# Turning q and k of chunks 4 to 11 by DMA transposes in place of TensorE, in a fused attention and feed-forward kernel

## The chip, the cores and the metric

One core of a Trainium2 chip. The experiments ran in three sets on three chips, and each ratio is to runs of the kernel before in the same set. The metric is device microseconds of one execution; lower is better.

## The reference

Attention over 4 batches, 8 heads, 768 positions, head size 64. A query sees the 8 global keys and the last 96 positions, with a distance bias per head. Its output, 3072 tokens by 512, goes through a feed-forward layer with a squared ReLU. Inputs and output are float32; the kernel computes in float16 with float32 sums.

```python
scores = scale * np.matmul(q, k.transpose(0, 1, 3, 2))
keep = is_global | ((rel >= 0) & (rel < n_local))          # 8 global keys, 96 local ones
scores = np.where(keep, scores + bias, -1e9)
a = softmax(scores)                                        # cut: written out in the reference
x = np.matmul(a, v).transpose(0, 2, 1, 3).reshape(3072, 512)
h = np.maximum(x @ w_in, 0.0)                              # w_in 512 x 2048
out = h * h @ w_out                                        # w_out 2048 x 512
```

## The kernel before

The work is cut into 12 chunks of 256 tokens. For each chunk the kernel loads q, k and v (GpSimd queue, cast to float16), turns q and k so that the head dimension lies on partitions, scores, attends, turns the attention output (`to_x`), and runs the two feed-forward products `first` and `second`. All engines but SyncE follow a fixed order: `place` puts the side jobs of a later chunk (attention, the turns) into numbered slots between the main feed-forward jobs.

The turn of q is eight 128x128 TensorE transposes into one PSUM bank, one ScalarE copy of 128x1024 to SBUF (the eviction), and two VectorE copies across partition halves. The turn of k is the same, followed by four small VectorE copies that build the keys of the neighbouring chunk.

```python
def turn_q(c, h0=0, h1=H, by=None):
    ck = chunks[c]
    ...                                     # cut: allocation of ck.q
    trp = bank([P, H, P], "trq", FP16)
    for h in range(h0, h1):
        nc.tensor.transpose(out=trp[:, h, :], in_=ck.sq[:, h, :], identity=ident)
    hh = slice(h0, h1)
    (by or nc.scalar.copy)(out=ck.q[:, 1, hh, :], in_=trp[:, hh, :])
    def beside():                           # runs just before the next job
        nc.vector.tensor_copy(out=ck.q[0:HP, 2, hh, :], in_=ck.q[HP:P, 1, hh, :])
        nc.vector.tensor_copy(out=ck.q[HP:P, 0, hh, :], in_=ck.q[0:HP, 1, hh, :])
    later.append(beside)
...
for c in range(1, NC):                      # one chunk period
    if c + 5 < NC:
        load(c + 5)
    main = zip_jobs(f2(c), f1(c + 1)) if c + 1 < NC else f2(c)
    side, slots = [], []
    if c + 3 < NC:
        side = [att[c + 3][i] for i in ORDER]
        slots = [0, 4, 5, 7, 8, 11, 12, 15]
    if c + 4 < NC:
        side += prep(c + 4) + [lambda c=c: fix_v(c + 4)]   # prep: turn_q, turn_k
        slots += [2, 9, 13]
    run(place(main, side, slots))
```

The softmax here doesn't subtract the row's maximum and nothing guards it: scores larger than these inputs give would overflow.

## Time and profile before

| | |
|---|---|
| median time | 240.03 us (239.79 to 240.20, 4 runs) |
| span in the profile | 239.2 us |
| TensorE, VectorE, ScalarE busy | 93%, 64%, 60% |
| period of one chunk, 80 to 185 us | 17.55 us |

The profile page of the kernel before. The first part gives busy time, share of the span and instructions. The rows of tenths cut the span into 40 slices of 6 us. The row that begins with 82% is the chain of work that ended last.

```profile
span 239.2 us, 5383 instructions
PE 221.9 (93%) x2214; PEld 155.1 (65%) x2214; DVE 152.4 (64%) x409; ACT 143.6 (60%) x256; POOL 38.6 (16%) x51
...
PE   4666988979899999999999999999999999999993
...
DMA  6999999994968159158249110110110111101112
...
q1 hardware_dynamic: 3456, 6.29, 6.8%
...
PE 82%; ACT 8%; DVE 6%; DMA 2%; issue 1%; POOL 0%; POOLq 0%
```

TensorE is full from about the twelfth slice to the end (busy 10.00 us in every stretch of 10 us from 70 to 230 us), and the chain is TensorE's. The DMA engines are busy for nine tenths or more from the second slice to the ninth, to about 54 us, while the weights and first chunks come in, and then busy in bursts. So each us of TensorE issue time after 70 us is a us of the kernel; other engines' work counts only where TensorE waits for it.

The groups of instructions that the change touches, in the kernel before: busy us and mean ns of one, then idle time before them.

```profile
L207 ACT COPY kx<-trk 128x1024 f16<-128x1024 f16 x11 | 11.8, 1069 | 0.8 <-PE trk L205 0.8
L192 ACT COPY qx<-trq 128x1024 f16<-128x1024 f16 x11 | 11.6, 1054 | 1.6 <-PE trq L190 1.6
...
L205 PE MATMUL trk<-ident,sk 128*128 128x128 f16 x96 | 8.2, 234 | 0.4 <-DMA sk<-in_k_dram 0.4
L190 PE MATMUL trq<-ident,sq 128*128 128x128 f16 x96 | 8.2, 234 | 2.0 <-DMA sq<-in_q_dram 2.0
```

A mean of 234 ns is not what a transpose costs: matmuls overlap, and the eight of one batch took 0.61 us together, not 8 x 0.234 = 1.87. The cost is what a batch delays. In the timeline of the kernel before (start, duration, instruction), the batch starts at 98.75 us and the next matmul at 99.19:

```profile
97.88 1.04 PE L329 MATMUL hps<-xt,w_in_sb 128*128 128x256 f16 x8
...
98.75 0.61 PE L190 MATMUL trq<-ident,sq 128*128 128x128 f16 x8
...
99.19 1.03 PE L341 MATMUL yps<-w_out_sb,h 128*128 128x512 f16 x4
```

That is 0.44 us for eight transposes, 55 ns each. One more place matters: the first period's handover to chunk 4, in the same timeline. The brackets give TensorE's idle time before an instruction and what ended it.

```profile
58.58 0.65 DVE L195 COPY qx<-qx 64x1024 f16<-64x1024 f16 x1 [0.69 <-ACT qx L192]
...
59.76 0.28 PE L304 MATMUL trx<-perm,tm 128*128 128x128 f16 x2
60.40 0.28 PE L304 MATMUL trx<-perm,tm 128*128 128x128 f16 x2 [0.36 <-DVE tm L292]
...
61.36 0.23 PE L261 MATMUL sp<-qx,kx 64*128 64x128 f16 x2 [0.67 <-ACT xt L306]
```

TensorE waited 0.36 us for tm and 0.67 us for ScalarE's xt, which came late because its own matmul had waited for that tm.

### The profile page before, as it was taken

Reading aid. Unit: us, or ns where it says so; the run is one execution under the profiler, and the core shown is the slowest. Engines: PE = TensorE matmul, PEld = TensorE weight load, DVE = VectorE, ACT = ScalarE, POOL = GpSimd, SP = SyncE. Lnnn points to the kernel's source line nnn. Section 1 sums busy time; section 2 is a strip of 40 time slices with the busy share of each in tenths; the row PEclk is TensorE's granted clock in tenths of the full one; section 3 lists DMA queues with packets and bytes.
Section 4 is the critical chain, followed back from the end, with each engine's and each line's share of the span. In section 5 each row is a group of like instructions: output and inputs, shape, how many; then the busy total and the mean of one; then the engine's idle time right before and its main releaser. Section 6 shows DMA issues by size and latency. Waiting matters only on the chain.

```text
span 239.2 us, 5383 instructions
## 1 busy us (share of the span) xinstructions
PE 221.9 (93%) x2214; PEld 155.1 (65%) x2214; DVE 152.4 (64%) x409; ACT 143.6 (60%) x256; POOL 38.6 (16%) x51
## 2 busy tenths in 40 slices
PE   4666988979899999999999999999999999999993
PEld 1554776846567767777676777767766676766651
DVE  7676689766967765567768755658758564333231
ACT  2975996957755764864764774784684564233310
POOL 8842534212302102102102000000000000000000
PEclk9999999999999999999999999999999999999998
DMA  6999999994968159158249110110110111101112
GB/s 61 192 193 203 192 207 187 182 181 83 167 98 84 51 89 91 48 87 88 57 79 90 44 47 0 47 45 3 44 47 0 47 45 47 43 1 47 44 44 88
DMA packets 45144, 20.26 MB, mean 85 GB/s; under 512 B 37952, under 2 KB 42048, under 8 KB 45120
## 3 DMA queue, kind: packets, MB, share of 16 engines
q0 software_dynamic: 41664, 13.63, 51.0%
q1 hardware_dynamic: 3456, 6.29, 6.8%
q8 instruction: 17, 0.28, 0.5%
q14 instruction: 7, 0.06, 0.1%
HBM read 27.26 MB, written 6.29 MB: 140 GB/s over the span
## 4 chain that ended last, share of the span: by engine, by line
PE 82%; ACT 8%; DVE 6%; DMA 2%; issue 1%; POOL 0%; POOLq 0%
PE yps L341 34%; PE hps L329 33%; PE sp L261 5%; PE av L285 4%; ACT ex L268 4%; PE trx L304 2%; DMA sq<-in_q_dram 2%; PE trq L190 2%; PE trk L205 2%; ACT hr L332 2%; DVE tm L292 1%; ACT kx L207 1%; ACT qx L192 1%; DVE qx L195 1%; DVE qx L196 1%
## 5 line engine op out<-in xcount | busy, mean ns | idle before, releaser
L329 PE MATMUL hps<-xt,w_in_sb 128*128 128x256 f16 x768 | 101.1, 276 | 0.0
L341 PE MATMUL yps<-w_out_sb,h 128*128 128x512 f16 x384 | 97.3, 379 | 0.0
L332 ACT ACTIVATE hr<-hps 128x512 f16<-128x512 f32 x96 | 58.9, 617 | 62.3 <-PE hps L329 58.0
L329 PEld LDWEIGHTS <-w_in_sb 128*128 128x128 f16 x768 | 72.7, 99 | 18.5 <-issue 0.2
L333 DVE TENSOR_TENSOR h<-hr 128x512 f16<-128x512 f16 x96 | 40.5, 422 | 43.9 <-ACT hr L332 43.4
L268 ACT ACTIVATE ex<-sp 128x512 f16<-128x512 f32 x96 | 49.4, 609 | 8.3 <-PE sp L261 8.3
L341 PEld LDWEIGHTS <-h 128*128 128x128 f16 x384 | 34.8, 98 | 26.6
L271 DVE TENSOR_TENSOR phat<-ex,mask 128x1024 f16<-128x1024 f16 x48 | 33.0, 691 | 20.7 <-ACT ex L268 20.7
L285 PEld LDWEIGHTS <-phat 128*128 128x128 f16 x384 | 18.8, 101 | 8.6 <-DVE phat L271 2.0
L292 DVE TENSOR_TENSOR tm<-av,rec 128x256 f16<-128x256 f32 x48 | 20.4, 425 | 1.7
L285 PE MATMUL av<-vodd,phat 128*128 128x65 f16 x256 | 18.5, 201 | 2.5 <-DVE vodd L238 1.5
L345 DVE COPY y<-yps 128x512 f32<-128x512 f32 x24 | 16.4, 685 | 5.4 <-PE yps L341 5.4
L306 ACT CAST xt<-trx 128x512 f16<-128x512 f32 x24 | 14.6, 608 | 8.5 <-PE trx L304 8.5
L261 PE MATMUL sp<-qx,kx 64*128 64x128 f16 x256 | 15.5, 232 | 2.9 <-DVE kx L207 1.3
L178 POOL DMA_DIRECT2D sq<-in_q_dram x12 | 10.7, 892 | 44.6 <-PE trq L190 40.3
L261 PEld LDWEIGHTS <-kx 64*128 64x128 f16 x256 | 10.5, 100 | 9.3 <-issue 6.8
L178 POOL DMA_DIRECT2D sk<-in_k_dram x12 | 10.5, 876 | 33.9 <-PE trk L205 29.1
L304 PE MATMUL trx<-perm,tm 128*128 128x128 f16 x96 | 10.6, 226 | 4.7 <-DVE tm L292 4.7
L304 PEld LDWEIGHTS <-tm 128*128 128x128 f16 x96 | 7.3, 99 | 8.8 <-DVE tm L292 6.2
L192 ACT COPY qx<-trq 128x1024 f16<-128x1024 f16 x11 | 11.6, 1054 | 1.6 <-PE trq L190 1.6
L207 ACT COPY kx<-trk 128x1024 f16<-128x1024 f16 x11 | 11.8, 1069 | 0.8 <-PE trk L205 0.8
L285 PE MATMUL av<-veven,phat 128*128 128x65 f16 x128 | 11.3, 194 | 0.0
(55 smaller groups left out, 132.5 us busy)
## 6 DMA issues: line engine op xcount, KB each, us to landing
out_dram<-y SPq DMA_DIRECT2D x24, 256.0 KB, 2.0
sq<-in_q_dram POOLq DMA_DIRECT2D x12, 256.0 KB, 6.3
sk<-in_k_dram POOLq DMA_DIRECT2D x12, 256.0 KB, 6.9
sv<-in_v_dram POOLq DMA_DIRECT2D x12, 256.0 KB, 7.5
w_in_sb<-in_moe_w_in_dram POOLq DMA_DIRECT2D x4, 512.0 KB, 12.2
w_out_sb<-in_moe_w_out_dram POOLq DMA_DIRECT2D x4, 512.0 KB, 17.2
```

Of the source, the lines that this page charges most:

```text
L178: nc.gpsimd.dma_start(out=dst, in_=src[ck.b, :, ck.u * CH:(ck.u + 1) * CH, :].rearrange("h (p e) d -> p h (e d)", e=2))
L261: nc.tensor.matmul(sp[ek][:, e, s, :], lhsT=ck.keys[rr][rows, h, :], rhs=ck.q[rows, 1 - ek:3 - ek, h, rr * HP:(rr + 1) * HP], start=True, ...
L268: nc.scalar.activation(out=ex[:, ek].rearrange("p e c -> p (e c)"), in_=sp[ek].rearrange("p e s c -> p (e s c)"), func=AF.Exp, scale=scale)
L271: later.append(lambda: nc.vector.tensor_tensor(out=phat, in0=ex, in1=mask[:, :, 2 * a:2 * a + 2, k0:k0 + 2, :].rearrange("p k e s c -> p k ...
L285: nc.tensor.matmul(av[:, e, rr, :], lhsT=phat[:, ek, e, s * P:(s + 1) * P], rhs=ck.vals[rr][:, 2 * a + e, ek, 0:D + 1], start=ek == 0, sto ...
L292: nc.vector.tensor_tensor(out=tm.rearrange("p r e d -> p e r d"), in0=av[:, :, :, 0:D], in1=rec[:, :, :, None].to_broadcast([P, 2, 2, D]), ...
L304: nc.tensor.matmul(trx[:, i, rr, :], lhsT=ck.tm[2 * g + i][:, rr, :, :], rhs=perm, start=True, stop=True)
L329: nc.tensor.matmul(hps[:, m2, :], lhsT=w_in_sb[:, kk, m * P:(m + 1) * P], rhs=ck.xt[:, kk, :], start=kk == 0, stop=kk == NCT - 1)
L332: nc.scalar.activation(out=hr, in_=hps, func=AF.Relu)
L333: later.append(lambda: nc.vector.tensor_tensor(out=ck.h2[:, 2 * i:2 * i + 2, :], in0=hr, in1=hr, op=ALU.mult))
L341: nc.tensor.matmul(ck.yps, lhsT=ck.h2[:, m, j * P:(j + 1) * P], rhs=w_out_sb[:, m, :], start=m == 0, stop=m == NFT - 1)
L345: nc.vector.tensor_copy(out=y, in_=ck.yps)
```

## The change

The intent is to take these transposes off the engine that bounds the kernel. For chunks 4 to 11, q and k are turned SBUF to SBUF by DMA transposes on SyncE's queue, which also carries the output stores. A pair is issued at the start of the period before the one that uses it, one to one and a half chunk periods ahead; loads are written one step earlier to match, and SyncE's queue gets a fixed order like the others.

```diff
+    def turn_dma(c):
+        ck = chunks[c]
+        new_q(c)
+        new_k(c)
+        nc.sync.dma_start_transpose(out=ck.q[:, 1], in_=ck.sq.rearrange("p h c -> p (h c)"))
+        nc.sync.dma_start_transpose(out=ck.k, in_=ck.sk.rearrange("p h c -> p (h c)"))
 ...
     def prep(c):
-        return [lambda: turn_q(c), lambda: turn_k(c)]
+        if c < NPE:                                      # NPE = 4
+            return [lambda: turn_q(c), lambda: turn_k(c)]
+        return [lambda: fix_q(c), lambda: fix_k(c)]      # VectorE copies only, as before
 ...
+    engines = {PE, ..., mybir.EngineType.SP}
 ...
-        load(5)
+        turn_dma(4)
+        load(6)
+        turn_dma(5)
         run(place(f2(0), ...))
         for c in range(1, NC):
             if c + 5 < NC:
-                load(c + 5)
+                turn_dma(c + 5)
+            if c + 6 < NC:
+                load(c + 6)
```

More of the change, by code (lines that the diff above doesn't have):

```diff
@@ L180, in load @@
                     "h (p e) d -> p h (e d)", e=2))
-    def turn_q(c, h0=0, h1=H, by=None):
-        ck = chunks[c]
-        if h0 == 0:
-            ck.q = qk_p.tile([P, 3, H, P], FP16, name="qx", tag="qx")
-        trp = bank([P, H, P], "trq", FP16)
-        for h in range(h0, h1):
-            nc.tensor.transpose(out=trp[:, h, :], in_=ck.sq[:, h, :], identity=ident)
-        hh = slice(h0, h1)
-        (by or nc.scalar.copy)(out=ck.q[:, 1, hh, :], in_=trp[:, hh, :])
-        def beside():
-            nc.vector.tensor_copy(out=ck.q[0:HP, 2, hh, :], in_=ck.q[HP:P, 1, hh, :])
-            nc.vector.tensor_copy(out=ck.q[HP:P, 0, hh, :], in_=ck.q[0:HP, 1, hh, :])
-        later.append(beside)
@@ L199, in turn_k, with new_q @@
-    def turn_k(c, h0=0, h1=H, by=None):
-        ck = chunks[c]
-        if h0 == 0:
-            ck.k = kx_p.tile([P, H, P], FP16, name="kx", tag="kx")
-        trp = bank([P, H, P], "trk", FP16)
-        for h in range(h0, h1):
-            nc.tensor.transpose(out=trp[:, h, :], in_=ck.sk[:, h, :], identity=ident)
-        hh = slice(h0, h1)
-        (by or nc.scalar.copy)(out=ck.k[:, hh, :], in_=trp[:, hh, :])
+    def new_q(c):
+        chunks[c].q = qk_p.tile([P, 3, H, P], FP16, name="qx", tag="qx")
@@ new lines, in new_k, with turn @@
+    def new_k(c):
+        chunks[c].k = kx_p.tile([P, H, P], FP16, name="kx", tag="kx")
+    def turn(st, dst, h0, h1, by):
+        trp = bank([P, H, P], "trp", FP16)
+        for h in range(h0, h1):
+            nc.tensor.transpose(out=trp[:, h, :], in_=st[:, h, :], identity=ident)
+        (by or nc.scalar.copy)(out=dst[:, h0:h1, :], in_=trp[:, h0:h1, :])
+    def turn_q(c, h0=0, h1=H, by=None):
+        if h0 == 0:
+            new_q(c)
+        turn(chunks[c].sq, chunks[c].q[:, 1], h0, h1, by)
+        later.append(lambda: fix_q(c, h0, h1))
@@ new lines, in turn_k, with fix_q @@
+    def turn_k(c, h0=0, h1=H, by=None):
+        if h0 == 0:
+            new_k(c)
+        turn(chunks[c].sk, chunks[c].k, h0, h1, by)
+        later.append(lambda: fix_k(c))
+    def turn_dma(c):
+        ck = chunks[c]
+        new_q(c)
+        new_k(c)
+        nc.sync.dma_start_transpose(out=ck.q[:, 1], in_=ck.sq.rearrange("p h c -> p (h c)"))
+        nc.sync.dma_start_transpose(out=ck.k, in_=ck.sk.rearrange("p h c -> p (h c)"))
+    def fix_q(c, h0=0, h1=H):
+        ck, hh = chunks[c], slice(h0, h1)
+        nc.vector.tensor_copy(out=ck.q[0:HP, 2, hh, :], in_=ck.q[HP:P, 1, hh, :])
+        nc.vector.tensor_copy(out=ck.q[HP:P, 0, hh, :], in_=ck.q[0:HP, 1, hh, :])
@@ L208, in turn_k, with fix_k @@
+    def fix_k(c):
+        ck = chunks[c]
         if ck.u == 0:
             ck.keys = (ck.k, ck.k)
-        else:
-            pre, zero = chunks[c - 1], chunks[c - ck.u]
-            kb = qk_p.tile([P, H, P], FP16, name="kb", tag="kb")
-            ck.keys = (kb, ck.k)
-            def change():
-                nc.vector.tensor_copy(out=kb[:, :, 0:HP], in_=ck.k[:, :, 0:HP])
-                nc.vector.tensor_copy(out=kb[:, :, HP + GP:P], in_=pre.k[:, :, HP + GP:P])
-                nc.vector.tensor_copy(out=kb[:, :, HP:HP + GP], in_=zero.k[:, :, 0:GP])
-                nc.vector.tensor_copy(out=ck.k[:, :, 0:GP], in_=zero.k[:, :, 0:GP])
-            later.append(change)
+            return
+        pre, zero = chunks[c - 1], chunks[c - ck.u]
+        kb = qk_p.tile([P, H, P], FP16, name="kb", tag="kb")
+        nc.vector.tensor_copy(out=kb[:, :, 0:HP], in_=ck.k[:, :, 0:HP])
+        nc.vector.tensor_copy(out=kb[:, :, HP + GP:P], in_=pre.k[:, :, HP + GP:P])
+        nc.vector.tensor_copy(out=kb[:, :, HP:HP + GP], in_=zero.k[:, :, 0:GP])
+        nc.vector.tensor_copy(out=ck.k[:, :, 0:GP], in_=zero.k[:, :, 0:GP])
+        ck.keys = (kb, ck.k)
@@ L371, in prep @@
     def prep(c):
-        return [lambda: turn_q(c), lambda: turn_k(c)]
-    engines = {PE, mybir.EngineType.Pool, mybir.EngineType.Activation, mybir.EngineType.DVE}
+        if c < NPE:
+            return [lambda: turn_q(c), lambda: turn_k(c)]
+        return [lambda: fix_q(c), lambda: fix_k(c)]
+    NPE = 4
+    engines = {PE, mybir.EngineType.Pool, mybir.EngineType.Activation, mybir.EngineType.DVE,
+               mybir.EngineType.SP}
     with tc.manual_schedule(engines=engines):
@@ L396 @@
              lambda: fill_decay(2, 3, 4, 8)])
+        load(4)
         ORD1 = (2, 3, 1, 6, 4, 5, 7)
@@ L399 @@
                   [2, 3, 4, 5, 6, 7, 8, 6, 7, 7]))
-        load(4)
+        load(5)
         run(place(f1(1), [att[2][i] for i in ORDER] + prep(3) + [lambda: fix_v(3)],
                   [0, 2, 3, 4, 5, 6, 7, 8, 6, 7, 7]))
-        load(5)
+        turn_dma(4)
+        load(6)
+        turn_dma(5)
         run(place(f2(0), [att[3][i] for i in ORDER] + prep(4) + [lambda: fix_v(4)],
```

## The prediction

> **What bounds the kernel.** TensorE. The page's first part has it busy 93% of a 239.2 us span; the table of 10 us stretches shows it busy 10.00 in every one from 70 to 230 us at a granted clock of 1.00, and the list of waits has none of TensorE from 85 to 150 us. Before 70 us it waits about 15 us in all. The chain that ended last is 82% TensorE. VectorE (64%), ScalarE (60%) and, after 60 us, the DMA engines have room.
>
> **What the change removes.** For chunks 4 to 11, 16 batches of eight TensorE transposes and their 16 ScalarE evictions of 128x1024. Matmuls overlap, so I price a batch by what it delays. In the timeline a trq batch starts at 98.75 us and the next matmul at 99.19; trk 106.66 to 107.10; trq 133.85 to 134.30; at 56.89 and 58.45 the distance is again 0.45. So 16 x 0.45 = 7.2 us, in stretches where TensorE is back to back. The evictions (1.06 us each, 17 us of ScalarE) are off the critical path after 70 us; near 57 to 61 us, where two waits of TensorE behind VectorE and ScalarE sum to 1.03 us, I count 0.3 us.
>
> **What it adds.** Sixteen SBUF-to-SBUF crossbar transposes of 256 KB on the SP queue, in one stream with the output stores, and new waits: VectorE's copies of qx and kx wait for a DMA, and later loads of sq and sk for the transposes that free their buffers. VectorE's work and Pool's order are unchanged.
>
> **Is it on the critical path?** The trace has no such DMA. [...] The kernel allows one pair per chunk period, 17.5 us now, about 16.6 after. A pair is issued at a period's start; its q is used some 18 us later, k some 25 us later. Up to about 8 us each nothing waits[...]. Chunk 4: its sq load is issued at 29.2 us, while DMA engines are 90% busy to about 50 us; its copy is due near 57 us. I expect it in time.
>
> **Prediction.** 240.07 - 7.2 - 0.3 = 232.6 us; range 231.3 to 238.5. Chances: faster by over 2% 0.72, within 2% 0.14, slower 0.14.
>
> **What would show each step right.** TensorE instructions fall by 128; the period falls from 17.5 to 16.6 us; TensorE stays 10 of 10 after 70 us without waits; ScalarE busy falls 17 us to about 127; the transposes land in at most 8 us each; VectorE's copy of qx waits for no DMA; loads from chunk 7 on are issued earlier, no longer waiting for TensorE.
>
> **What would make it wrong.** Transposes of over 8 us (by themselves, or sharing engines with small-packet loads): VectorE waits at the qx copy, TensorE at sp, and the time rises above 236. Loads or stores slowed by them, so that y buffers run out. Chunk 4 or 5 late near 57 to 65 us: a one-time loss of a few us. [...]

The marked cuts are what the author took one DMA transpose to need, the outcome that hung on it, and a remark on the clock; no trace here shows them. The sum, 240.07 - 7.2 - 0.3 = 232.6 us, has no term for the transposes. That these stay hidden rested on the 8 us of the text, about half a period of 16.6 us, and on leads of 18 and 25 us; that they would land in 8 us was the author's estimate, from no measurement.

## More of the kernel before

Times of the kernel before scatter by up to 0.8% within a set (239.1 to 241.05 us in the last one), so differences under about 1 us are read from traces (one per kernel, two of the changed one), from a fixed event onward, and not from medians.

## The result

The changed kernel took 233.52 us in the median (232.75 to 233.58, 4 runs) against 240.03 us. The ratio is 0.9722, with a 95% interval of 0.9700 to 0.9744. A ratio here is the mean time of one kernel's runs over the mean of the other's in the same rounds, so it is not quite the ratio of the medians. The result was correct.

The same lines of the page of the changed kernel:

```profile
span 231.8 us, 5156 instructions
PE 214.7 (93%) x2086; PEld 147.9 (64%) x2086; DVE 152.6 (66%) x409; ACT 129.5 (56%) x240; POOL 38.7 (17%) x51
...
PE   4666997979899999999999999999999999999993
...
DMA  6999999999999999993510811410011011100112
...
q1 hardware_dynamic: 20352, 10.49, 21.0%
...
PE 77%; ACT 9%; DVE 8%; DMA 2%; issue 2%; POOL 0%; POOLq 0%
```

TensorE has 128 instructions fewer and is still the bound: 93% of a shorter span. The DMA row is what changed character: nine tenths or more from the second slice to the 18th, of 5.8 us each, to about 104 us, where it was so to about 54. No busy TensorE slice shows this. The period fell from 17.55 to 16.66 us.

The DMA issues by line in the changed kernel (count, then median us from issue to landing), and the span of landings of the q transposes:

```profile
qx<-sq SPq DMA_TRANSPOSE x8, 6.1
kx<-sk SPq DMA_TRANSPOSE x8, 5.7
```

```profile
DMA to landing us min/median/max: 2.7/6.1/10.2
```

The whole list of VectorE's waits in the changed kernel contains no DMA at all (waited for: us in total, times, longest):

```profile
DVE h L344 <- ACT hr L343: 42.4, 51, 1.3
DVE phat L282 <- ACT ex L279: 20.4, 43, 1.5
DVE y L356 <- PE yps L352: 5.4, 3, 2.8
DVE kb L227 <- ACT kx L194: 1.0, 1, 1.0
DVE qx L194 <- PE trp L193: 0.9, 1, 0.9
DVE tiny L105 <- PEq L454: 0.8, 1, 0.8
DVE qx L217 <- ACT qx L194: 0.3, 1, 0.3
```

So every transpose landed before its first reader was ready, though some took over 10 us.

The profiled spans differ by 7.4 us and the means by 6.7. The profiled run of the kernel before was a long one (241.05 us, where the four timed ones took 239.79 to 240.20), and over the later runs its span ranged from 237.3 to 239.3 us. In the traces (that of e10_chunk3 left out) the first second-layer group began between 48.67 and 50.01 us, so the start scatters by more than 1 us; that it makes the whole difference is not shown. The chains that ended last, from the first second-layer group of chunk 0 to the last group (start, us, what), are steadier. Before:

```profile
49.95 1.83 PE yps L341 x8
...
228.70 6.92 PE yps L341 x32
```

After:

```profile
49.77 1.83 PE yps L352 x8
...
221.25 6.92 PE yps L352 x32
```

From that first event to the end of the span the kernel before takes 239.2 - 49.95 = 189.25 us and the changed one 231.8 - 49.77 = 182.03, a gain of 7.22 us. A second trace of the changed kernel gave 231.8 - 49.80 = 182.00. This "time from 50 us" is used for all small differences below. The granted TensorE clock, 1.00 at full speed, was 1.00 from 50 to 227 us in the traces of both kernels, and 0.9 or more in every slice from 50 to 220 us of the pages of the other runs, apart from the stage told under e10_chunk3.

The handover to chunk 4 in the timeline of the changed kernel, where the copy of qx no longer waits:

```profile
57.75 0.42 DVE L217 COPY qx<-qx 64x1024 f16<-64x1024 f16 x1
...
59.62 0.28 PE L315 MATMUL trx<-perm,tm 128*128 128x128 f16 x2 [0.65 <-DVE tm L303]
...
60.17 0.23 PE L272 MATMUL sp<-qx,kx 64*128 64x128 f16 x2 [0.27 <-DVE kx L230]
```

From the first event to these first scores of chunk 4 it is 60.17 - 49.77 = 10.40 us, and 61.36 - 49.95 = 11.41 us before. So 1.01 us of the gain falls here, and 7.22 - 1.01 = 6.21 us in the rest, where 14 of the 16 batches were: 0.44 us each. TensorE's two waits here hardly shrank (1.03 us before, 0.65 + 0.27 = 0.92 after): with two batches fewer it reaches VectorE's results sooner. What the 1.01 us comes from is left to e2_pe_back.

### The profile page after: what moved, and what is told of

Its sections match the earlier page's. It is cut to its first block, busy times and chain, and to the rows that moved or that the text cites. A ratio compares the mean times of both kernels' runs of the same rounds, so it can differ in the third digit from the quotient of the medians. Undisturbed runs are those within 1.5% of the kernel's fastest.

```text
span 231.8 us, 5156 instructions
## 1 busy us (share of the span) xinstructions
PE 214.7 (93%) x2086; PEld 147.9 (64%) x2086; DVE 152.6 (66%) x409; ACT 129.5 (56%) x240; POOL 38.7 (17%) x51
## 4 chain that ended last, share of the span: by engine, by line
PE 77%; ACT 9%; DVE 8%; DMA 2%; issue 2%; POOL 0%; POOLq 0%
PE yps L352 35%; PE hps L340 31%; PE sp L272 5%; ACT ex L279 4%; PE av L296 4%; PE trx L315 2%; DMA sq<-in_q_dram 2%; DVE tm L303 2%; ACT hr L343 2%; ACT mask L136 1%; ACT kx L194 1%; DVE h L344 1%; DVE phat L282 1%; DVE qx L217 1%; DVE qx L218 1%
## 5 line engine op out<-in xcount | busy, mean ns | idle before, releaser
L343 ACT ACTIVATE hr<-hps 128x512 f16<-128x512 f32 x96 | 58.3, 611 | 68.0 <-PE hps L340 63.6
L279 ACT ACTIVATE ex<-sp 128x512 f16<-128x512 f32 x96 | 49.4, 609 | 8.0 <-PE sp L272 7.9
L178 POOL DMA_DIRECT2D sq<-in_q_dram x12 | 10.7, 891 | 41.4 <-DMA qx<-sq 33.1
L272 PEld LDWEIGHTS <-kx 64*128 64x128 f16 x256 | 10.5, 101 | 9.1 <-issue 6.8
L178 POOL DMA_DIRECT2D sk<-in_k_dram x12 | 10.5, 876 | 11.3 <-DMA kx<-sk 5.7
L178 POOL DMA_DIRECT2D sv<-in_v_dram x12 | 10.8, 900 | 3.1 <-DMA w_out_sb<-in_moe_w_out_dram 1.4
L272 PE MATMUL sp<-qx,kb 64*128 64x128 f16 x128 | 9.4, 222 | 0.0
```

Source lines behind the costliest of these rows:

```text
L178: nc.gpsimd.dma_start(out=dst, in_=src[ck.b, :, ck.u * CH:(ck.u + 1) * CH, :].rearrange("h (p e) d -> p h (e d)", e=2))
L272: nc.tensor.matmul(sp[ek][:, e, s, :], lhsT=ck.keys[rr][rows, h, :], rhs=ck.q[rows, 1 - ek:3 - ek, h, rr * HP:(rr + 1) * HP], start=True, ...
L279: nc.scalar.activation(out=ex[:, ek].rearrange("p e c -> p (e c)"), in_=sp[ek].rearrange("p e s c -> p (e s c)"), func=AF.Exp, scale=scale)
L343: nc.scalar.activation(out=hr, in_=hps, func=AF.Relu)
```

## The experiments

Theory A: the gain is TensorE's issue time, and the transposes are hidden. Rival B: the gain is ScalarE's relief, or the new order of loads. Rival C: the transposes cost something hidden and eat part of the gain. The parts of the change were undone or done alone, all on the same footing: five rounds, or three where noted. Each figure under "from 50 us" is that run's span less the start of its first second-layer group.

### a0_after: the changed kernel again

No edit.

> The changed kernel again, as the base of this set, five rounds. Theory A (the gain is TensorE issue time alone, 16 batches x 0.45 us): ratio to before 0.970, 7.2 us less. If something the change adds costs TensorE time, or a part of the gain is lost, the ratio stays near 0.973 or above (6.5 us less). The profiled spans differ by 7.4 us, the first timed medians by 6.5.

Measured: 233.66 us against 240.34, ratio 0.9718 (0.9698 to 0.9737). The ratio repeats the first one and is between the two expectations, with 0.970 inside its interval; timing alone cannot choose. From 50 us the gain is 7.2 us, so nothing of that size is lost after the start.

### e1_half: half of the dose

```diff
-    NPE = 4
+    NPE = 8          # and no turn_dma for chunks 4 to 7
```

> Only chunks 8 to 11 turned by the DMA, chunks 4 to 7 by TensorE. Theory A, a dose of 8 batches: 240.0 - 3.6 = 236.4, half of what the whole change gains in this set. Rival C (what the transposes gain while loads still crowd the DMA engines, chunks 4 to 7, is partly lost): more than half of the gain remains with chunks 8 to 11 alone, 236.0 or less.

Measured: 237.15 us, ratio 0.9864 (0.9844 to 0.9884), which by ratios is 3.3 us of 6.8. From 50 us: 235.0 - 49.32 = 185.68, a gain of 3.57 us, or 8 x 0.446. In chunk 4's handover nothing is gained (11.42 us, as before), because chunk 4's eviction is still there. Half the batches give half the gain; crowding by loads does not eat what chunks 4 to 7 bring. That it is so exactly half is partly chance: the other 3.65 us are the 1.01 us of the handover and six batches, not eight, as e2_pe_back shows next.

### e2_pe_back: TensorE's time put back

```diff
+    def idle_turns():
+        trp = bank([P, H, P], "trp", FP16)
+        for h in range(H):
+            nc.tensor.transpose(out=trp[:, h, :], in_=zero[:, 0:P], identity=ident)
-        return [lambda: fix_q(c), lambda: fix_k(c)]
+        return [lambda: (fix_q(c), idle_turns()), lambda: (fix_k(c), idle_turns())]
```

> The changed kernel with 16 idle batches of eight TensorE transposes put back at the old places (of a tile of zeros, into a bank that nobody reads): TensorE's time is back, the ScalarE copies are not. Theory A: back to before, 240.0 within 0.7. Rival B (the gain is ScalarE's relief of 17 us or the earlier loads): stays near 233.5.

Measured: 239.39 us, ratio 0.9954 (0.9933 to 0.9975): most of the gain is gone, and about 1 us stays, a little outside the 0.7 expected. From 50 us: 238.3 - 50.01 = 188.29, so 0.96 us of gain stays. The timeline of this kernel shows where:

```profile
59.83 0.39 PE L315 MATMUL trx<-perm,tm 128*128 128x128 f16 x4
60.41 0.23 PE L272 MATMUL sp<-qx,kx 64*128 64x128 f16 x2 [0.20 <-DVE kx L230]
```

Chunk 4's handover takes 60.41 - 50.01 = 10.40 us, as in the changed kernel, although both of its TensorE batches are back. So, with the evictions gone, the two batches there are worth nothing: TensorE's waits are 0.20 us here and 0.92 without the batches. The 1.01 us goes with the eviction of trq, for which VectorE waits no more. The batches taken out with that eviction kept were not tried. The other 14 batches are worth the remaining 188.29 - 182.03 = 6.3 us.

The loads go out early in this kernel too (q of chunk 11 at 99.0 us; 98.0 in the changed kernel, 117.2 before), and the 6.3 us are lost all the same. So the second half of Rival B, the earlier loads, falls here.

### e3_act_back: ScalarE's time put back

```diff
+    def idle_copy():
+        dst = tm_p.tile([P, H, P], FP16, name="idle", tag="idle", bufs=2)
+        nc.scalar.copy(out=dst, in_=mask[:, 0, :, 0, :])
-        return [lambda: fix_q(c), lambda: fix_k(c)]
+        return [lambda: (fix_q(c), idle_copy()), lambda: (fix_k(c), idle_copy())]
```

> The changed kernel with 16 idle ScalarE copies of 128x1024 put back at the old places, TensorE's transposes not. Theory A: no more than 0.5 us over the changed kernel of this set. Rival B: back by several us towards 240.

Measured: 233.10 us, ratio 0.9694 (0.9672 to 0.9717). From 50 us: 230.7 - 48.67 = 182.03, exactly the changed kernel's, and the handover takes 59.07 - 48.67 = 10.40 us again. The idle copies took 1.08 and 1.10 us in this trace where checked, as the evictions had, but read SBUF and held no PSUM bank. So the time of these copies on ScalarE is worth nothing; what counted in chunk 4's stage was a wait in VectorE's queue. Rival B's first half falls.

### e4_order_only: the orders without the transposes

```diff
-    engines = {PE, ...Pool, ...Activation, ...DVE}
+    engines = {PE, ...Pool, ...Activation, ...DVE, mybir.EngineType.SP}
-            if c + 5 < NC: load(c + 5)
+            if c + 6 < NC: load(c + 6)      # and loads 4 to 6 one stage earlier
```

> The kernel before with only the orders of the change: loads written one stage earlier and SyncE's queue in fixed order, all transposes on TensorE. Theory A: the same as before, within 0.5 us, since TensorE waits for no load after 20 us. Rival (the orders bring part of the gain): 1 us or more under before.

Measured: 240.54 us, ratio 1.0012 (0.9988 to 1.0036); from 50 us 239.0 - 49.69 = 189.31 against 189.25. The handover is as before too, 61.10 - 49.69 = 11.41 us. The orders are worth nothing by themselves. This run does not test earlier loads, though: its staging buffers still wait for TensorE's transposes, and q of chunk 11 is loaded at 117.0 us, as before. That test is e2_pe_back.

### e5_late: a shorter lead (three rounds)

```diff
         turn_dma(4)
         load(6)
-        turn_dma(5)
-            if c + 5 < NC: turn_dma(c + 5)
+            if c + 4 < NC: turn_dma(c + 4)
```

> The changed kernel with each pair from chunk 5 on issued one chunk period later, at the start of the period in whose slot 2 the q copy is due. Landing took 2.7 to 10.5 us in the changed kernel's trace and slot 2 comes some 2 us after the issue, so VectorE should now wait 1 to 8 us for the DMA at the copy of qx, in order, and TensorE after it: 3 to 20 us over the changed kernel, most of it in the periods of chunks 5 to 7 where loads crowd the DMA engines. If the lead is of no matter: unchanged.

Measured: 235.41 us, ratio 0.9801 (0.9780 to 0.9823). By ratios that is 0.9% or 2 us over the changed kernel, less than the 3 us expected. From 50 us: 233.5 - 49.77 = 183.73, 1.7 us over. The wait that was expected is there, in VectorE's list of waits:

```profile
DVE qx L217 <- DMA qx<-sq: 5.7, 5, 2.3
```

It is small because the transposes were quicker: the median landing of q fell to 2.9 us from 6.1. The page's DMA row fits this:

```profile
DMA  6999999999979379593596720410511011100112
```

A load of q waits for the transpose that frees its staging buffer. A later transpose therefore holds the loads back too (GpSimd waited five times for q transposes in both traces, 54.8 us in all against 33.1 in the changed kernel), the DMA engines are less crowded (134 GB/s from 60 to 80 us, against 186), and the late transpose meets fewer loads. That the crowding set the landing time is read from these traces; it was not forced separately. The lead is worth 1.7 us, not the 3 to 20 that I computed from landings in another kernel's crowding.

### e6_double: twelve more transposes

```diff
+        for src in (ck.sq, ck.sk) if c >= 6 else ():
+            idle = qk_p.tile([P, H, P], FP16, name="idle", tag="idle", bufs=2)
+            nc.sync.dma_start_transpose(out=idle, in_=src.rearrange("p h c -> p (h c)"))
```

> The changed kernel with every transpose of chunks 6 to 11 issued a second time into a tile that nobody reads (12 more of 256 KB in the same queue). Theory A (the transposes are hidden and the queue has room, a pair needs about 6 us of a 16.7 us period when no loads run, 20 us in the crowded stretch but two periods of slack): no change from the changed kernel within 0.5 us. If the transposes already sit near the path, or disturb TensorE through memory traffic: 1 us or more over it.

Measured: 233.93 us, ratio 0.9733 (0.9711 to 0.9754), within the noise of the changed kernel's 0.9718; from 50 us 232.2 - 49.92 = 182.28, 0.25 us over. The transposes are off the path and the queue has room for nearly twice as many. Rival C falls, for anything above a few tenths of a us; only chunks 6 to 11 were doubled, and chunks 4 and 5 rest on the list of waits above.

### e7_x_dma: a further turn moved

```diff
+    def to_x_dma(c):                        # chunks 3 to 11
+        ck.xt = h_p.tile([P, NCT, CH], FP16, name="xt", tag="xt", bufs=4)
+        nc.sync.dma_start_transpose(out=ck.xt.rearrange("p a (r c) -> p (a r) c", r=2),
+                                    in_=ck.tmx.rearrange("p a r e d -> p (a r e d)"))
 ...                                        # cut: tm kept in one tile; this job in slot 13, not 15
-            nc.sync.dma_start(out=out[r0:r0 + P, :], in_=y)
+            rows = out[r0:r0 + P, :].rearrange("(p e) d -> e p d", e=2)
+            for e in range(2):
+                nc.sync.dma_start(out=rows[e], in_=y[e * HP:(e + 1) * HP, :])
```

> A further step of the same kind: the turn of the attention output (eight 128x128 matmuls a chunk, which also put the tokens in order, and two ScalarE copies) is done for chunks 3 to 11 by one crossbar transpose a chunk, and the order of tokens by the output stores, each in two halves. By theory A a batch of four delays the next matmul by 0.23 us (130.36 to 130.58, 140.66 to 140.89 in the trace of before): 18 x 0.225 = 4.1 us, so 233.6 - 4.1 = 229.5. Under 229 if the wait of trx for tm (0.65 us in chunk 3's stage) goes too; over 231 if the queue falls behind.

Measured: correct, 230.95 us (230.37 to 233.15), ratio 0.9639 (0.9600 to 0.9678). It beats the changed kernel, by less than expected. The traced run took 233.11 us and is one of the two slow ones of six: its span is 229.8 us, where four runs have 228.0 to 228.7. From 50 us in it: 229.8 - 49.99 = 179.81, a gain of 2.2 us where 4.1 was expected. Two parts are missing. The last TensorE group ends at 218.02 + 6.92 = 224.94, and the span 4.9 us later; in the changed kernel it is 221.25 + 6.92 = 228.17 and 3.6 us. So the end is 1.2 us longer. And chunk 4's handover did not shorten (10.53 us against 10.40): with the trx matmuls gone, TensorE only reached its wait for VectorE earlier.

```profile
60.52 0.23 PE L272 MATMUL sp<-qx,kx 64*128 64x128 f16 x2 [1.65 <-DVE kx L230]
```

Up to the last group the gain is 171.48 - 168.03 = 3.45 us; with the 0.13 lost at the handover, the other 16 batches gave 3.6, or 0.22 each, as read from the trace of before.

### e8_tail: the same with whole stores at the end

```diff
-    NX = 3                      # chunks 3 to 11
+    BYDMA = range(3, 11)        # chunk 11 by matmul, its stores whole
```

> As e7_x_dma, but chunk 11 keeps its matmul turn, so that the last two stores are whole again. In the trace of e7_x_dma the last TensorE work ends 4.9 us before the end, in the changed kernel 3.6 us: this should give 1.2 us back at the end for 0.45 us of TensorE, 0.8 us in all: some 230.1, and no more runs at 233. If the split stores do not cause the longer end, it is 0.45 us slower than e7_x_dma.

Measured: 230.76 us (230.20 to 231.01), ratio 0.9614 (0.9585 to 0.9643). The page and the chain of this kernel:

```profile
span 228.1 us, 5053 instructions
```

```profile
217.57 6.92 PE yps L365 x32
```

The end is 228.1 - 224.49 = 3.6 us again. From 50 us: 228.1 - 49.22 = 178.88, 0.93 us under the trace of e7_x_dma. But that trace is of a slow run. The spans of e8_tail, 228.1 to 228.9 us, are no shorter than the 228.0 to 228.7 of the other four of e7_x_dma (on another chip), and the medians differ by 0.2 us where 0.8 was expected. No run came out at 233 (two of six had before). So the split stores may be what made the end longer in those runs; a cost of 1.2 us in every run is not shown.

### e9_early: VectorE's copies of chunk 4 placed earlier

```diff
-                  [0, 2, 3, 4, 5, 6, 7, 8, 6, 7, 7]))   # last three: fix_q, fix_k, fix_v of chunk 4
+                  [0, 2, 3, 4, 5, 6, 7, 8, 5, 5, 7]))
```

> As e8_tail, with VectorE's copies of q and k of chunk 4 placed one or two jobs earlier, where nothing that TensorE is about to read waits behind them: the wait of sp for kx in chunk 4's stage (1.65 us in e7_x_dma) should fall to some 0.5 us, with up to 0.5 us of it coming back at av of chunk 4: 0.5 to 1 us under e8_tail. No change if the chain of VectorE there only moves its wait.

Measured: 230.35 us, ratio 0.9593 (0.9566 to 0.9620), not separable from e8_tail. From 50 us: 228.3 - 49.20 = 179.10, 0.2 us over it. The list of TensorE's waits shows that the wait only moved: sp for kx fell from 1.5 to 0.9 us, and av for phat rose by as much. In e8_tail:

```profile
PE sp L272 <- DVE kx L230: 1.5, 1, 1.5
...
PE av L296 <- DVE phat L282: 0.6, 1, 0.6
```

In e9_early:

```profile
PE av L296 <- DVE phat L282: 1.2, 2, 0.6
PE sp L272 <- DVE kx L230: 0.9, 1, 0.9
```

TensorE waits for VectorE in that stage in both orders tried. The expected 0.5 to 1 us is not there.

### e10_chunk3: one chunk earlier (three rounds)

```diff
-    NPE = 4
+    NPE = 3
         load(5)
+        turn_dma(3)
         run(place(f1(1), ...))
```

> The changed kernel with chunk 3 turned by the DMA as well, as early as its order allows. Its loads are issued at 25 to 26 us and land late in the crowded stretch, a transpose there took 8 to 10 us, and the copy of q is due at 46.6 us: VectorE should wait for the DMA some 2 to 6 us and the time rise by 1 to 5 us over the changed kernel, not fall by the 0.9 us of its two batches.

Measured: 239.43 us, ratio 0.9972 (0.9939 to 1.0004). By ratios that is 2.6% or 6 us over the changed kernel, slightly worse than the 1 to 5 us expected: nearly the whole gain is gone. In the timeline of VectorE, and then in the list of TensorE's waits:

```profile
49.36 0.42 DVE L217 COPY qx<-qx 64x1024 f16<-64x1024 f16 x1 [3.54 <-DMA qx<-sq]
```

```profile
PE trx L315 <- DVE tm L303: 8.6, 8, 5.1
```

Chunk 3's load is issued at about 25 us and lands 15.1 to 15.6 us later among the weights (read in the traces of before and after), and the transpose needs some 9 us more, so it is ready at 49.4 us for a copy that VectorE reached at 45.8. VectorE stops, then TensorE, for 5.1 us at one stroke and 0.9 us more for the transpose of k. Then comes a cost that was not expected. The table of stretches of this kernel (stretch and length, busy time of TensorE, its weight loads, VectorE, ScalarE and GpSimd, then granted TensorE clock, DMA share, GB/s):

```profile
44.00:46.00 2.00, 1.83 (x24) 1.43 (x21) 1.35 (x5) 1.55 (x4) 0.00 (x0) 1.00 1.60 179
...
52.50:57.20 4.70, 4.63 (x29) 2.24 (x30) 1.39 (x2) 2.06 (x4) 2.50 (x3) 0.50 1.49 170
```

After the idle of 5.1 us the granted clock is 0.50 for some 6 us, from 51.0 to 57.2: the first second-layer group takes 3.60 us in the timeline, against 1.90 in the changed kernel. That the idle brought the lower clock was not tested by a run of its own. Of the loss, 3.8 us lie before the first second-layer group (53.61 against 49.77) and 2.0 us after it, of which that group's slow pace alone is 1.7.

## Why the prediction was right

The predicted 232.6 us is 0.9 us under the measured median, and the range held it.

- *TensorE bounds, and a batch costs what it delays.* Shown. Half the batches gave half the gain (e1_half: 3.57 us for 8), putting TensorE's work back took 6.3 us of the gain away (e2_pe_back), putting ScalarE's back took nothing (e3_act_back). The listed mean of 234 ns for each transpose would have promised 30 us for 128 of them; 55 ns was the right price. As forecast, TensorE was busy 10.00 us in every stretch of 10 us from 70 to 220.
- *16 x 0.45 = 7.2 us.* Mis-sized by 1.0: 14 x 0.44 = 6.2. The two batches of chunk 4 lay in a stage where TensorE waits for VectorE a moment later, and there e2_pe_back shows that, with the evictions gone, they were worth nothing. The prediction said that all lay "in stretches where TensorE is back to back"; for these two that failed.
- *0.3 us for the evictions near 57 to 61 us.* By the same reading mis-sized the other way: 1.0 us. VectorE's in-order wait for one eviction had been delaying everything behind it. The two errors nearly cancel, which is luck: 7.5 predicted, 7.22 from 50 us on. Whichever way the stage of chunk 4 is divided, it was to give 0.9 + 0.3 = 1.2 us and gave 1.01.
- *The transposes are hidden.* Shown, for a wider margin than claimed. "At most 8 us each" was wrong: they took 2.7 to 10.5 us to land. But the closest of them, k of chunk 4, was issued at 46.1 us, landed 10.2 us later and was first copied at 59.5, 3.2 us after that, and e6_double shows room for 12 more. The queue did not fall behind: from chunk 5's on, each pair had landed before the next was issued (at 63.4 us for 63.8, at 75.8 for 78.2), and from 93 us on, when few or no loads ran, they landed in 2.7 to 3.9 us.
- *ScalarE falls by 17 us.* The listed evictions did; busy time fell by 14.1 us (143.6 to 129.5), since instructions overlap in it: two of 0.61 us each take 1.09 together in its timeline.
- *Loads from chunk 7 on are issued earlier.* Right: the load of q for chunk 11 went out at 98.0 us against 117.2. It was worth nothing in time (e2_pe_back has the early loads and loses the gain), and with the transposes the DMA engines were full for longer (to 104 us against 54).
- *The rest of the gap,* 6.7 us by means against 7.2 by traces, is within the scatter of the span of the kernel before, 237.3 to 239.3 us. Its cause was not looked into.

What one transpose cost here. Eight 128x128 blocks in one DMA instruction, 256 KB from SBUF to SBUF, landed in 2.7 to 3.9 us when issued from 93 us on, with few or no loads running, and in 7.5 to 10.5 us when issued from 44 to 81 us, in the stretch crowded with loads. SyncE was occupied for 1.25 to 1.8 us of each of the first kind, and for up to 4.0 us when the engines were crowded. On TensorE eight blocks delayed the next matmul by 0.44 us, 55 ns each. A stretch of 7 us of the changed kernel, 111 to 118 us, in 40 slices of 0.175 us; a store of 256 KB was issued just before, then the pair for chunk 9:

```profile
GB/s 0 0 0 0 0 304 410 374 269 183 262 293 291 288 275 47 0 16 234 297 287 293 287 85 0 47 0 0 0 0 0 0 0 0 0 0 0 0 0 0
...
qx<-sq SPq DMA_TRANSPOSE x1, 2.8
kx<-sk SPq DMA_TRANSPOSE x1, 2.8
```

The first four busy slices add up to about 240 KB and should be the store; the two groups after it, of 287 and 262 KB, are the transposes. In their full slices they move 262 to 297 GB/s, where the store reaches 410. Of the 2.8 us to landing, the bytes move in little more than 1.

## What to carry to other kernels

Price work on a full engine by what it delays, not by its listed duration (here 55 ns, not 234), and ask for each piece whether the engine waits just after it: there it may be worth nothing, as in chunk 4's stage (10.40 us with its two batches and without, once the evictions were gone). Before moving work to the DMA queue, set its landing time *in the traffic of that stage* against the lead that is free: here 10 us was no harm at leads of 13 to 18 us, and the same transpose one chunk earlier cost nearly the whole gain, part of it at a granted clock of 0.50 after a wait of 5.1 us. The move can be repeated while lead lasts: turning the attention output in the same way (e8_tail, 230.76 us, ratio 0.9614) beats both kernels. Whether the stores at the very end must stay whole for that is not shown.
